# Sparse attention with two feed-forward layers in one launch: weight pieces three half-pieces ahead, a PSUM bank for the sums of squares, half-size weight loads and a planner with new latencies

## The chip, the cores and the metric

The kernel runs on one core of one Trainium2 chip. The metric is the device time of one execution in microseconds; the time before is the median of three runs. Engines are named as in the profile: PE is TensorE (PEld its weight loads), DVE is VectorE, ACT is ScalarE, POOL is GpSimd, SP is SyncE, which here issues all DMAs.

## What is computed

Top-32 attention over 4 batches of 8 heads, 576 rows of 64, and then two feed-forward layers over the 2304 rows. All inputs come in 64-bit floats.

```python
scores = scale * np.matmul(q, k.transpose(0, 1, 3, 2))
kth = np.partition(scores, -top_k, axis=-1)[..., -top_k:-top_k + 1]
scores = np.where(scores >= kth, scores, -1000000000.0)
attn = np.exp(scores - np.max(scores, axis=-1, keepdims=True))
attn = attn / (np.sum(attn, axis=-1, keepdims=True) + 1e-09)
x = np.matmul(attn, v)          # heads side by side: 2304 x 512
h = x @ w_in                    # 512 x 2048
x = np.maximum(0.01 * h, h) @ w_out
h = x @ w_in2
out = (h * (1.0 / (1.0 + np.exp(-h)))) @ w_out2
```

## The kernel before

The 2304 rows are cut into 18 blocks of 128 rows (one row block of each two batches is shared, 64 rows each), and a block's 8 heads into 4 pairs, so that attention has 72 pairs. A pair goes through: scores on PE (L760, into S), a copy to SBUF on ACT (L772), the search for the 32nd largest value on DVE (4 rounds of MAX8 and 3 of MATCH_REPLACE8 for each of the two heads, L784 to L788), bias on POOL (L798), cut and exponential on ACT (L810, L818), a split of the weights p into two 16-bit halves (ACT L833, POOL L841), a DMA transpose (L850) and the product with v on PE (L866). After 4 pairs a block is normed, split and transposed into xT, and the layers take it in quanta of 12 matmuls of 128x512 each: 4 quanta h0 (L978, from xT), 4 quanta o0 (L1031, into acc), the same again for layer 2 (h1 from yT, o1). Every product of two 32-bit values is made of 16-bit halves: high by high, high by low, low by high.

The weights are four matrices of a million values (w_in, w_out, w_in2, w_out2), each in 8 pieces of 128x1024. A piece is loaded as raw 64-bit words (L432), then ACT takes the upper word (L439), the top bits of the lower word are shifted down by ACT or DVE ("shift", L467 or L464), and DVE joins both ("join", L476), which gives a 32-bit float y. PE adds up the squares of all pieces (L493), DVE takes the trace and a scale (L503), and each piece is then scaled and split into a high half (ACT, L521 or L523) and a low half, made by DVE (L528) or by POOL (L533, behind a scaling by ACT L538 or POOL L540). All of this lies in one tile, w_all, in slots of 2048 16-bit columns: a piece's y lies one slot above the slot of its halves, so that the halves of piece g overwrite y of piece g-1. Raw words lie in free slots further up; the last two pieces of w_out2 go through 256-column loads into the one buffer `of`, and shifts of w_out2 into the three `g` buffers. Squares of q, x and the output of layer 1 (L682, L916) write into `junk`, a PSUM bank that only takes what nobody reads; the sums of squares of the weights use the PSUM tile `acc` of the second matmul.

The order of all instructions is set by a planner (Plan.run): operations are added with an engine, a duration, a latency and their names; the planner simulates five engines and the DMA queue, takes for each engine the candidate of the highest rank (the length of what depends on it, with PACE, plus BOOST) among those that can start within SLACK of the earliest, with LATE added to the readiness of some; the instructions are then issued engine by engine in that order, and nothing overtakes on an engine at run time. AHEAD holds layer 1 at most three blocks ahead of layer 2.

Of the kernel before, what the change touches and what calls it, by code (L numbers as in the profile page):

```python
# [31 lines left out]
NRAW = 4  # L32
W_AFTER = (("ktr", 0, 0), ("qtr", 0, 0))

W_MID = (
    ("ACT", "DVE", "ACT", "ACT", "ACT", "ACT", "ACT", "ACT"),
    ("ACT", "ACT", "ACT", "ACT", "ACT", "ACT", "ACT", "DVE"),
    ("ACT", "ACT", "ACT", "ACT", "ACT", "ACT", "DVE", "DVE"),
    ("ACT", "ACT", "DVE", "ACT", "ACT", "ACT", "ACT", "DVE"),
)  # L40
W_LO = (
    ("DVE", "ACT", "ACT", "ACT", "DVE", "ACT", "DVE", "ACT"),
    ("DVE", "ACT"),
    ("DVE", "ACT", "DVE", "POOL", "DVE", "ACT", "DVE", "POOL"),
    ("DVE", "ACT", "DVE", "ACT", "DVE", "ACT", "DVE", "ACT"),
# [1075 lines left out]
```

## Time and profile before

| | before |
|---|---|
| time, median of 3 runs (lowest to highest) | 1101.1 us (1099.29 to 1101.45) |
| profiled execution, its own time | 1101.91 us |
| its span, first to last instruction | 1100.1 us |
| busy: PE, DVE, ACT, POOL | 957.0, 896.0, 823.2, 637.4 us |
| mean granted clock of PE | 0.938 |
| HBM read, written | 47.71 MB, 4.72 MB |

The page gives busy time by engine; a group of instructions shows its count, busy time, mean duration and the idle time of its engine ahead of it with what ended it. Names in the rows: m and w are the search's tiles, sb the copied scores, ph and pT the split and transposed weights of attention, hl and gT the same of the layers, h and acc the layers' PSUM tiles.

### The profile page before, as it was taken

What the parts mean: (1) busy time and instruction counts of PE and PEld (TensorE: products, weight loads), DVE (VectorE), ACT (ScalarE), POOL (GpSimd) and SP (SyncE); (2) the same over time, 40 slices, a digit from 0 to 9 for tenths busy, and PEclk for the clock granted to TensorE, in tenths of its full rate; (3) what the DMA queues carried; (4) which work ended last, traced back from release to release, by engine and by line L of the source; (5) the groups of instructions that cost most, each with busy time, mean ns of one, the idle gap of its engine ahead of it and who ended that gap; (6) DMA issues with size and microseconds to landing.
All of it is one profiled execution on the core that took longest, in us unless ns stands there. A gap on an engine that the chain in (4) does not pass through costs nothing.

```text
span 1100.1 us, 19543 instructions
## 1 busy us (share of the span) xinstructions
PE 957.0 (87%) x6824; PEld 486.4 (44%) x6824; DVE 896.0 (81%) x1853; ACT 823.2 (75%) x1235; POOL 637.4 (58%) x913
## 2 busy tenths in 40 slices
PE   2434735668999999999999999999999999999998
PEld 1223313334554544544544545445454545444443
DVE  4999989998948999999999999994899999951010
ACT  5999998778866887878988778786787878662322
POOL 1355656567774776665876576665666665552321
PEclk9655867788999999999999999999999999999999
DMA  7997878553975687678888687687567766574432
GB/s 216 311 313 227 197 221 211 103 111 67 162 137 111 133 151 148 112 130 148 165 149 145 118 155 123 128 143 139 117 126 126 146 123 122 102 129 63 76 64 58
DMA packets 458115, 157.53 MB, mean 143 GB/s; under 512 B 440864, under 2 KB 449056, under 8 KB 455968
## 3 DMA queue, kind: packets, MB, share of 16 engines
q1 hardware_dynamic: 458016, 156.29, 70.0%
q8 instruction: 53, 0.87, 0.3%
q14 instruction: 46, 0.38, 0.1%
HBM read 47.71 MB, written 4.72 MB: 48 GB/s over the span
## 4 chain that ended last, share of the span: by engine, by line
PE 49%; DVE 20%; ACT 11%; issue 7%; POOL 6%; DMA 5%; SPq 1%; ACTq 0%; POOLq 0%; DVEq 0%
PE acc L1031 21%; PE h L978 20%; DVE w L786 7%; DVE m L788 6%; PE S L760 3%; PE pv L866 3%; POOL ph L841 2%; DMA pT<-ph 2%; ACT sb L818 2%; DVE w_all L476 2%; DVE m L784 1%; ACT sb L810 1%; POOL hl L1012 1%; ACT w_all L439 1%; PE acc L493 1%
## 5 line engine op out<-in xcount | busy, mean ns | idle before, releaser
L1031 PE MATMUL acc<-w_all,gT 128*128 128x512 f16 x1728 | 400.4, 382 | 12.8 <-ACT w_all L523 5.5
L788 DVE MAX8 m<-w 128x8 f32<-128x576 f32 x432 | 307.6, 746 | 0.0
L1012 POOL TENSOR_TENSOR hl<-g,hl 128x512 f16<-128x512 f32 x144 | 174.5, 1212 | 149.1 <-ACT hl L1005 132.3
L1031 PEld LDWEIGHTS <-gT 128*128 128x128 f16 x1728 | 166.3, 99 | 205.4 <-issue 18.3
L841 POOL TENSOR_TENSOR ph<-sb,ph 128x1152 f16<-128x1152 f32 x72 | 171.1, 2377 | 124.8 <-ACT ph L833 114.3
L786 DVE MATCH_REPLACE8 w<-m,w 128x576 f32<-128x576 f32 x288 | 212.1, 742 | 0.0
L978 PE MATMUL h<-w_all,xT 128*128 128x512 f16 x864 | 200.7, 384 | 12.7 <-DMA xT<-hlx 11.7
L978 PE MATMUL h<-w_all,yT 128*128 128x512 f16 x864 | 197.0, 381 | 0.6 <-DVE g L996 0.6
L760 PE MATMUL S<-k,qT 128*128 128x64 f16 (+3 forms) x640 | 94.2, 309 | 51.7 <-ACT sb L772 28.9
L978 PEld LDWEIGHTS <-xT 128*128 128x128 f16 x864 | 84.5, 99 | 113.9 <-DMA xT<-hlx 12.4
L818 ACT ACTIVATE sb<-sb,nb,u 128x576 f32<-128x576 f32 x144 | 122.5, 862 | 15.9 <-POOL nb L798 9.6
L978 PEld LDWEIGHTS <-yT 128*128 128x128 f16 x864 | 84.2, 98 | 99.5 <-issue 2.4
L996 DVE SCALAR_TENSOR_TENSOR g<-g,h 128x512 f32<-128x512 f32 x72 | 49.1, 682 | 95.9 <-ACT g L991 94.0
L810 ACT ACTIVATE sb<-sb,m 128x576 f32<-128x576 f32 x144 | 108.8, 764 | 24.4 <-DVE m L788 24.3
L772 ACT ACTIVATE sb<-S 128x1152 f32<-128x1152 f32 x72 | 81.0, 1125 | 46.5 <-POOL ph L841 44.7
L1005 ACT ACTIVATE hl<-g 128x512 f16<-128x512 f32 x144 | 89.8, 624 | 29.8 <-DVE g L996 25.0
L784 DVE MAX8 m<-sb 128x8 f32<-128x576 f32 x144 | 101.9, 745 | 6.4 <-ACT sb L772 6.3
L786 DVE MATCH_REPLACE8 w<-m,sb 128x576 f32<-128x576 f32 x144 | 105.9, 742 | 0.0
L866 PEld LDWEIGHTS <-pT 128*128 128x128 f16 (+1 forms) x2400 | 81.4, 104 | 29.1 <-DMA pT<-ph 13.7
L866 PE MATMUL pv<-v,pT 128*128 128x65 f16 (+3 forms) x2400 | 85.3, 199 | 9.4 <-DMA pT<-ph 9.3
L798 POOL TENSOR_SCALAR nb<-m,u 128x1 f32<-128x1 f32 x144 | 63.6, 445 | 49.3 <-DVE m L788 46.7
L760 PEld LDWEIGHTS <-qT 128*128 128x128 f16 (+1 forms) x640 | 44.5, 106 | 100.8 <-issue 45.6
(99 smaller groups left out, 1005.9 us busy)
## 6 DMA issues: line engine op xcount, KB each, us to landing
w_all<-in_moe_w_in_dram SPq DMA_DIRECT2D x16, 1024.0 KB, 6.3
w_all<-in_moe_w_out_dram SPq DMA_DIRECT2D x14, 1024.0 KB, 6.0
raw<-in_k_dram SPq DMA_DIRECT2D x16, 256.0 KB, 3.8
rawq<-in_q_dram SPq DMA_DIRECT2D x32, 128.0 KB, 2.8
raw<-in_v_dram SPq DMA_DIRECT2D x16, 256.0 KB, 3.1
out_dram<-of SPq DMA_DIRECT2D x16, 256.0 KB, 2.4
gT<-hl SPq DMA_TRANSPOSE x144, 3.2
of<-in_moe_w_out_dram SPq DMA_DIRECT2D x8, 256.0 KB, 2.8
```

Source lines behind the costliest of these rows:

```text
L760: nc.tensor.matmul(out=t[p0:p1, o:o + k1 - k0], lhsT=lhs, rhs=kt[:, k0:k1], start=(x == 0), stop=(x == 1),)
L784: nc.vector.max(m[:, 0], T[sbk][:, h])
L786: nc.vector.match_replace(w, m[:, step // 2], T[sbk][:, h] if step == 1 else w, NEG)
L788: nc.vector.max(m[:, step // 2], w)
L810: nc.scalar.activation(out=x, in_=x, func=AF.Prelu, scale=-1.0, bias=T["m", s][:, h, 3, 7:8], alpha=2.0**-CUT)
L818: nc.scalar.activation(out=x, in_=x, func=AF.Exp, scale=T["u", blk, hf][:, 1, p % 2:p % 2 + 1], bias=T["nb", s][:, h:h + 1],)
L841: nc.gpsimd.tensor_tensor(out=T[phk][:, 1, x0 * S:x1 * S], in0=T[sbk][:, x0:x1].rearrange("p h k -> p (h k)"), in1=T[phk][:, 0, x0 * S:x1 ...
L866: nc.tensor.matmul(out=o[p0:p1, 0:d1 - d0], lhsT=pT[:, c, p0:p1], rhs=T["v", b, p][:, vc, d0:d1], start=(i == 0), stop=(i == len(mm) - 1),)
L978: nc.tensor.matmul(out=t, lhsT=a[:, ai], rhs=w_rhs(layer, wi, kk, i), start=(n == 0), stop=(n == 3 * KDM - 1))
L1005: nc.scalar.activation(out=n[:, 0], in_=T[gk], func=AF.Copy)
L1012: nc.gpsimd.tensor_tensor(out=n[:, 1], in0=T[gk], in1=n[:, 0], op=ALU.subtract)
L1031: nc.tensor.matmul(out=t, lhsT=g[:, ai], rhs=w_rhs2(layer, wi, 4 * i + j), start=(i == 0 and j == 0 and n == 0), stop=(i == NCH - 1 and j ...
```

## The change

It changes seven things.

1. **Slots.** w_all is addressed in half-slots of 1024 columns. A piece's y now lies three half-slots (6 KB) above its halves, raw words in half-slots 51 to 66. The high half of piece g waits for the low half of piece g-2, the low half for that of g-1; so two pieces can be in work at once.
2. **Shift in place.** The shifted bits are written into the raw tile itself, in every second 32-bit word, by ACT, DVE or now POOL (from the 16-bit word, as ACT does).
3. **Who does what.** Tables W_MID, W_HI and W_LO: of the shifts of 1024 columns ACT had 20 and DVE 4; now ACT has 7, DVE 10, POOL 7. Of 512 columns ACT had 10, DVE 2; now ACT 2, DVE 4, POOL 7. Of 256: ACT 4, DVE 4; now POOL 6. DVE makes 18 low halves for 15, POOL 14 for 17; ACT scales 9 pieces for 15, POOL 5 for 2; POOL makes 3 of the 32 high halves. Joins on DVE: 24 of 1024, 12 of 512, 8 of 256 before; 24, 13 and 6 after.
4. **Loads.** 512 columns at a time (67 weight loads for 38), from the start of the program; the rest of w_out2 is staged in two `k` and `v` buffers in place of `of`; loads of k and v behind the first block wait until all weight loads are issued; the planner issues a weight load only when the DMA queue is within 0.5 us of empty.
5. **PSUM.** `junk` goes; a bank `gram` holds the sums of squares, which run piece by piece for all four matrices. Squares of q and x go into qT and xT, those of layer 1's output into `of`.
6. **Constants.** w_consts and u2 are made in two parts: layer 2's h needs the scales of three matrices only.
7. **Planner.** New durations and latencies; BOOST, PACE and LATE with other numbers and more names; NUDGE, a rank for single operations; TAIL and HOP for the time from an end to a waiting engine; a rule that an instruction of DVE on the list PORT, when POOL is busy by more than STALL, counts as starting at POOL's end, and POOL's next instruction as waiting for it.

```diff
-    "raw": 2, "rawq": 2, "g": 3, "of": 1, "hlk": 1, "hlx": 1, "hl": 2, "gT": 3, "xT": 1, "yT": 2, "xf": 1,
+    "raw": 2, "rawq": 2, "g": 2, "of": 1, "hlk": 1, "hlx": 1, "hl": 2, "gT": 3, "xT": 1, "yT": 2, "xf": 1,
...
-W_AFTER = (("ktr", 0, 0), ("qtr", 0, 0))
...
 BOOST = {
-    "g2": 200, "comb": 200, "norm": 200, "ylo": 200, "xlo": 200, "kvscale": 200, "wtrace": 200,
+    "g2": -1639, "comb": 1589, "norm": -1649, "ylo": 1315, "xlo": 583, "kvscale": -335, "wtrace": 200,
...
+NUDGE = {
+    290: -4105, 1074: -2255, 1097: -2285, 1239: -1961, 1818: -1479, 1200: 1526, 673: -1232, 923: -1982,
...
+TAIL = {"PE": 0.16, "ACT": 0.09, "DVE": 0.085, "POOL": 0.03, "SP": 0.0}
+HOP = {"PE": 0.055, "ACT": 0.036, "DVE": 0.036, "POOL": 0.085, "SP": 0.08}
+PORT = ("wjoin", "wlo", "kvlo", "xlo", "qlo", "wmid")
+STALL = 0.09
+AHEAD_DMA = 0.5
...
+                        if o.heavy:
+                            u = max(u, dma_free - AHEAD_DMA)
+                            t = max(t, dma_free - AHEAD_DMA)
+                        if e == "DVE" and o.port and clock["POOL"] > u + STALL:
+                            u = clock["POOL"]
+                        elif e == "POOL" and port_end > t:
+                            u, t = max(u, port_end), port_end
...
-    junk = ps.tile([128, 512], F32, name="junk", tag="junk", bufs=1)
+    gram = ps.tile([128, 128], F32, name="gram", tag="gram", bufs=1)
...
-    w_all = wp.tile([128, (4 * NWP + 1) * 2 * WP], F16, name="w_all")
+    w_all = wp.tile([128, (8 * NWP + 3) * WP], F16, name="w_all")
...
     def w_f32(i, c):
-        return w_at(NWP * i + c + 1).bitcast(F32)
+        return w_at(2 * (NWP * i + c) + 3, 2).bitcast(F32)
...
+                def mid(n=n, c=c, raw=raw):
+                    t = raw().rearrange("p (n t) -> p n t", t=2)[:, :, 0]
+                    m16 = raw().bitcast(U16).rearrange("p (n t) -> p n t", t=4)[:, :, 1]
+                    if mid_on(c) == "DVE":
+                        nc.vector.tensor_scalar(t, t, 29, None, op0=ALU.logical_shift_right)
+                    elif mid_on(c) == "POOL":
+                        nc.gpsimd.tensor_scalar(t, m16, 2.0**-13, -0.4999, op0=ALU.mult, op1=ALU.add)
...
-            yn = [n for d in (range(NWP) if i > 1 and c == 0 else [c]) for n in w_names(d)]
-            add("PE", 0.5, square, r=yn, w=[("gram", i)], new=[("acc", ("gram", i))] if c == 0 else [], name=f"gram{i}")
+            add("PE", 0.46, square, r=w_names(c), w=["gram"], name=f"gram{i}", seq="gram")
...
+            add(hi_on(c), 0.96 if hi_on(c) == "ACT" else 1.2, hi, r=yn + [("ws", i), ("wlo", g - 2)], w=[("whi", g)], name=f"whi{i}")
+            add("POOL" if plain else "DVE", 2.12 if plain else 1.19, lo,
+                r=[("ws", i), ("whi", g), ("wlo", g - 1)], w=yn + [("wlo", g), ("w", i, c)], name=f"wlo{i}")
...
-                out=junk[:, 0:256], in_=T[rk].rearrange("p h d -> p (h d)"), func=AF.Square,
```

How it moves instructions, at three places. First DVE at the start of the program, behind v's first low half: L642 and L694 split k and v, L476 and L532 are joins, L464 and L520 shifts, L784 and L836 the first step of the first search. Before:

```order
L642 SCALAR_TENSOR_TENSOR v<-raw,sv_75,v 128x9x64
L356 TENSOR_SCALAR fx<-h 128x1
L357 TENSOR_SCALAR sk_71<-fx 128x1
L358 TENSOR_SCALAR sk_71<-fx 128x1
L784 MAX m_187<-sb 128x8 x2
L642 SCALAR_TENSOR_TENSOR hlk<-raw,sk_71,hlk 128x9x64
```

After:

```order
L694 SCALAR_TENSOR_TENSOR v<-raw,sv_75,v 128x9x64
L532 SCALAR_TENSOR_TENSOR w_all<-w_all 128x1024
L766 SCALAR_TENSOR_TENSOR hlx<-rawq,qs,hlx 128x4x64 x2
L520 TENSOR_SCALAR w_all<-w_all 128x1024
L411 TENSOR_SCALAR fx<-h 128x1
L412 TENSOR_SCALAR sk_71<-fx 128x1
L413 TENSOR_SCALAR sk_71<-fx 128x1
L532 SCALAR_TENSOR_TENSOR w_all<-w_all 128x1024
```

The first search stood right behind the second scale of k; now joins and shifts stand ahead of it, four and three by the time it comes (two of them ahead of these rows).

Second, DVE at the first joins of w_out2. Before:

```order
L357 TENSOR_SCALAR sv_76<-fx 128x1
L358 TENSOR_SCALAR sv_76<-fx 128x1
L476 SCALAR_TENSOR_TENSOR w_all<-w_all,g 128x512 x3
L464 TENSOR_SCALAR g<-w_all 128x512 x2
L476 SCALAR_TENSOR_TENSOR w_all<-w_all,g 128x512 x3
```

After (L550 is the trace of w_in2, L586 a low half):

```order
L520 TENSOR_SCALAR w_all<-w_all 128x512
L532 SCALAR_TENSOR_TENSOR w_all<-w_all 128x512
L836 MAX m_1208<-sb 128x8
L550 SCALAR_TENSOR_TENSOR gram,wtot<-gram,ident 128x128
L836 MAX m_1208<-sb 128x8
L532 SCALAR_TENSOR_TENSOR w_all<-w_all 128x512 x2
L586 SCALAR_TENSOR_TENSOR w_all<-w_all,ws_911 128x1024
L532 SCALAR_TENSOR_TENSOR w_all<-w_all 128x512 x4
```

Three joins and three more stood there with two shifts between; now there are one, two and four, with search steps, a trace and a low half between them.

Third, SP at the start of the program, where L432 and L500 load weights, L597, L601, L649 and L653 load k and v, L673 and L725 q. Before:

```order
L597 DMA raw<-in_k_dram 128x2x256
L601 DMA raw<-in_k_dram 64x64 x2
L673 DMA rawq<-in_q_dram 128x4x64
L597 DMA raw<-in_v_dram 128x2x256
L601 DMA raw<-in_v_dram 64x64 x2
L673 DMA rawq<-in_q_dram 128x4x64
L660 DMA_TRANSPOSE k<-hlk 128x9x128
```

After:

```order
L500 DMA w_all<-in_moe_w_in_dram 128x1024
L649 DMA raw<-in_k_dram 128x2x256
L653 DMA raw<-in_k_dram 64x64 x2
L500 DMA w_all<-in_moe_w_in_dram 128x1024
L725 DMA rawq<-in_q_dram 128x4x64
L649 DMA raw<-in_v_dram 128x2x256
L653 DMA raw<-in_v_dram 64x64 x2
L500 DMA w_all<-in_moe_w_in_dram 128x1024
```

The first weight load stood behind the first transposes and the second k and v; now it is the first DMA, and one stands between each of the others.

## Rows read from the trace of the kernel before

**Rows 1.** The page, busy time of each engine, share of the span, instructions

```profile
PE 957.0 (87%) x6824; PEld 486.4 (44%) x6824; DVE 896.0 (81%) x1853; ACT 823.2 (75%) x1235; POOL 637.4 (58%) x913
```

**Rows 2.** Three stretches by windows; each engine's busy time, clock, DMA

```profile
core 0: us, PE busy (x) PEld busy (x) DVE busy (x) ACT busy (x) POOL busy (x), PEclk, DMA share, GB/s
0.00:297.90 297.90, 168.16 (x1247) 96.15 (x1248) 269.03 (x509) 251.71 (x349) 170.08 (x216) 0.78 0.75 195
297.90:976.40 678.50, 668.87 (x4972) 335.11 (x4972) 614.89 (x1326) 531.29 (x822) 431.54 (x657) 1.00 0.74 133
976.40:1100.10 123.70, 120.01 (x608) 55.18 (x606) 12.06 (x20) 40.18 (x65) 35.76 (x41) 1.00 0.41 72
```

**Rows 3.** PE's timeline around 257 and 297 us: start, us, line, idle before

```profile
257.57 2.08 PE L760 MATMUL S<-k,qT 128*128 128x512 f16 x8 [5.19 <-ACT sb L772]
...
296.67 1.21 PE L760 MATMUL S<-k,qT 128*64 128x512 f16 x16
```

**Rows 4.** The chain of waits, 170 to 300 us: start, us, what

```profile
243.63 5.01 PE acc L493 x64
...
285.32 2.59 PE h L978 x12
```

**Rows 5.** Groups of DVE's instructions to 297.9 us: busy, mean ns, idle before

```profile
L476 DVE SCALAR_TENSOR_TENSOR w_all<-w_all 128x1024 int32<-128x1024 int32 x24 | 32.5, 1362 | 0.1
...
L528 DVE SCALAR_TENSOR_TENSOR w_all<-w_all,ws 128x1024 f16<-128x1024 f32 x15 | 24.0, 1602 | 1.8 <-ACT w_all L523 1.8
L476 DVE SCALAR_TENSOR_TENSOR w_all<-w_all,g 128x512 int32<-128x512 int32 x12 | 10.3, 891 | 5.3 <-ACT g L467 5.1
L476 DVE SCALAR_TENSOR_TENSOR w_all<-w_all,g 128x256 int32<-128x256 int32 x8 | 9.0, 1124 | 0.1
...
L464 DVE TENSOR_SCALAR g<-of 128x256 int32<-128x256 int32 x4 | 3.5, 882 | 0.0
...
L464 DVE TENSOR_SCALAR w_all<-w_all 128x1024 int32<-128x1024 int32 x4 | 2.7, 684 | 0.0
...
L464 DVE TENSOR_SCALAR g<-w_all 128x512 int32<-128x512 int32 x2 | 0.8, 422 | 0.0
```

**Rows 6.** The same lines: duration ns min/median/max, first and last start

```profile
L476 DVE SCALAR_TENSOR_TENSOR w_all<-w_all x24: 1193/1210/3084, 23.8 to 150.4; 128x1024 int32<-128x1024 int32 x24
L476 DVE SCALAR_TENSOR_TENSOR w_all<-w_all,g x20: 403/690/2414, 159.9 to 228.0; 128x512 int32<-128x512 int32 x12, 128x256 int32<-128x256 int32 x8
...
L528 DVE SCALAR_TENSOR_TENSOR w_all<-w_all,ws x15: 1259/1278/2437, 68.2 to 276.6; 128x1024 f16<-128x1024 f32 x15
...
L464 DVE TENSOR_SCALAR g<-of x4: 285/666/1910, 208.6 to 225.4; 128x256 int32<-128x256 int32 x4
```

**Rows 7.** DVE's timeline: start, us, line, and the idle time before it

```profile
17.35 0.16 DVE L356 TENSOR_SCALAR fx<-h 128x1 int32<-128x1 int32 x1 [5.30 <-PE h L551]
...
159.91 2.83 DVE L476 SCALAR_TENSOR_TENSOR w_all<-w_all,g 128x512 int32<-128x512 int32 x3 [5.13 <-ACT g L467]
...
173.15 1.29 DVE L476 SCALAR_TENSOR_TENSOR w_all<-w_all,g 128x512 int32<-128x512 int32 x2
...
297.10 0.75 DVE L788 MAX8 m<-w 128x8 f32<-128x576 f32 x1
```

**Rows 8.** Groups of POOL's instructions to 297.9 us

```profile
L533 POOL TENSOR_TENSOR w_all<-w_all 128x1024 f16<-128x1024 f32 x17 | 37.4, 2200 | 27.1 <-ACT w_all L521 24.9 <-issue 2.0
...
L540 POOL TENSOR_TENSOR w_all<-w_all,ws 128x1024 f32<-128x1024 f32 x2 | 4.4, 2204 | 0.0
```

**Rows 9.** Groups of ACT's instructions to 297.9 us

```profile
L467 ACT ACTIVATE w_all<-w_all 128x1024 int32<-128x1024 uint16 x20 | 22.4, 1123 | 3.2 <-DMA w_all<-in_moe_w_in_dram 3.0 <-DVE w_all L476 0.2
```

**Rows 10.** Who waited for whom, DVE to 297.9 us: total, times, longest

```profile
DVE fx L356 <- PE h L551: 12.6, 5, 5.8
...
DVE junk L503 <- PE acc L493: 2.2, 2, 1.8
```

**Rows 11.** The page, DMA issues: KB each, us to landing

```profile
w_all<-in_moe_w_in_dram SPq DMA_DIRECT2D x16, 1024.0 KB, 6.3
```

More of the change, by code (lines that the diff above doesn't have):

```diff
@@ L80 @@
+SLACK = {
+    "PE": 0.03, "ACT": 0.14, "DVE": 0.08, "POOL": 0.02, "SP": 0.1,
+}
 STATS = {}
@@ L86 @@
 class Op:
-    __slots__ = ("n", "eng", "dur", "lat", "dma", "fn", "new", "use", "pred", "succ", "bl", "left", "ready", "t0", "t1", "name", "soft", "stage", "slot")
+    __slots__ = ("n", "eng", "dur", "lat", "dma", "fn", "new", "use", "pred", "succ", "bl", "left", "ready", "t0", "t1", "name", "soft", "stage", "slot", "port", "tr", "heavy")
 class Plan:
@@ L159, in run @@
         engines = ("PE", "ACT", "DVE", "POOL", "SP")
-        clock = {e: 0.0 for e in engines}
+        turn = False
+        clock = {e: 0.7 for e in engines}
         busy = {e: 0.0 for e in engines}
         dma_free = 0.0
+        port_end = 0.0
         cand = {e: [] for e in engines}
@@ L177, in run @@
             best = None
-            for e in engines:
+            for e in ("PE", "ACT", "POOL", "DVE", "SP") if turn else engines:
                 lst = []
@@ L398, in w_rows, with w_units @@
         return w_bits[i][kk * 128:(kk + 2) * 128, :].rearrange("(k p) d -> p k d", p=128)
-    def slot(j):
-        return ("slot", j)
+    RAW3 = (53, 55, 57, 59, 61, 63, 65, 59, 61, 63, 65, 63, 65)
+    STAGE = ("k", "v")
+    def w_units(i, c):
+        if i < 3:
+            return [(0, WP, 51 + 4 * (c % 4))]
+        out = []
+        for h in range(2):
+            n = 2 * c + h
+            if n < len(RAW3):
+                out.append((512 * h, 512, RAW3[n]))
+            else:
+                out += [(512 * h + o, 256, STAGE[o // 256 % 2]) for o in (0, 256)]
+        return out
     def w_ops(i):
@@ new lines, in w_ops, with load @@
+                step = min(n, 512)
+                for o2 in range(0, n, step):
+                    def load(o=o, o2=o2, n=n, c=c, home=home, rk=rk, raw=raw, step=step):
+                        if home == "k":
+                            T[rk] = tile_of(rk, "k", [128, 9 * 128], F16)[:, 0:1024].bitcast(I32)
+                        elif home == "v":
+                            T[rk] = tile_of(rk, "v", [128, 10 * VW], F16)[:, 0:1024].bitcast(I32)
+                        nc.sync.dma_start(out=raw()[:, 2 * o2:2 * (o2 + step)], in_=w_rows(i, c, o + o2, step))
+                    k = o2 // 512 * 2
+                    add("SP", 0.42, load, w=rn[k:k + 2] + tn[k:k + 2], new=rnew, lat=2.4, dma=2.7 * step / WP,
+                        name=f"wload{i}", seq="wload", mark="wlast")
@@ new lines, in w_ops, with join @@
+                add(mid_on(c), {"DVE": 0.08 + 0.52 * n / WP, "ACT": 0.1 + 0.92 * n / WP, "POOL": 0.1 + 1.1 * n / WP}[mid_on(c)], mid,
+                    w=tn, name=f"wmid{i}")
+                def join(o=o, n=n, c=c, raw=raw):
+                    y = w_f32(i, c).bitcast(I32)[:, o:o + n]
+                    t = raw().rearrange("p (n t) -> p n t", t=2)[:, :, 0]
+                    nc.vector.scalar_tensor_tensor(
+                        out=y, in0=y, scalar=3, in1=t, op0=ALU.logical_shift_left, op1=ALU.bitwise_or
+                    )
```

398 lines of the change are left out of this document (196 added, 202 removed), and 10 rows, old and new, of tables (BOOST, LATE).

## The prediction

> **What bounds the kernel now.** I began with the shares on the page: PE is busy for 87% of the span and DVE for 81% [rows 1]. Neither number decides anything, since both are averages, so next I cut the span at two instants of DVE's timeline. One is 297.9 us, where DVE ends the top-32 search of pair 17 (a pair is one 128-row block with two heads; there are 72). The other is 976.4 us, where it ends pair 72. The reader should compare the three rows [rows 2]. Before 297.9, PE works for 168 of 298 us at a mean granted clock of 0.78 (it moves between the two levels 1.2 and 2.4 GHz), while DVE works for 269.0. After it, PE has 668.9 of 678.5 and then 120.0 of 123.7, at clock 1.00. So the last 802 us are PE's own work: 788.9 of 802.2 busy, some 13 us to be had there by anyone. The first 298 us are DVE's. That DVE is 615 of 678 busy in the middle matters little: its waits there are for PE.
>
> The timeline of PE joins the two stretches [rows 3]. Its last long wait, 5.19 us before the scores at 257.6, is for the copy of earlier scores; from there it runs without a gap. A quantum (12 matmuls of 512 columns, either layer's h or acc) costs 2.59 us, as the chain of waits shows [rows 4]. There are 288. In the listed order of PE's instructions 29 stand ahead of the scores of pair 18 (at 296.7). So a microsecond that DVE saves before pair 18 is worth a microsecond at the end, as long as PE's order keeps about the same number of quanta behind that point. In the changed order 28 stand ahead instead of 29: one quantum more is left, **+2.6 us**.
>
> **DVE up to pair 17.** 269.0 busy and 28.9 idle. The change doesn't touch the search. It touches the weights: 7 groups of rows, 32.5+24.0+10.3+9.0+3.5+2.7+0.8 = 82.8 us [rows 5]. How much of it is work? The smallest durations say [rows 6]: a join of 1024 takes 1.193, one of 256 0.403, a low half 1.259, a shift of 256 0.285; two joins of 512 in 1.29 give 0.645 [rows 7]; shifts of 1024 and 512 have tight means, 0.684 and 0.422 [rows 5]. Alone, the present work is 24x1.193 + 12x0.645 + 8x0.403 = 39.5 for joins, 15x1.259 = 18.9 for low halves, 4x0.684 + 2x0.422 + 4x0.285 = 4.7 for shifts: 63.1. The other 19.7 us are instructions that were stretched (a join took up to 3.084).
>
> The change makes joins 24x1.193 + 13x0.645 + 6x0.403 = 39.4, low halves 18x1.259 = 22.7, shifts 10x0.684 + 4x0.422 = 8.5: 70.6, **+7.5 us**. DVE gets more work, not less. The shifts now write every second word in place; no row shows this. If the stride halved their rate, they would cost 8.5 more. I take no change, since they already read with that stride; the 8.5 stays in the range.
>
> **The stretch.** What becomes of the 19.7? In the big joins it is 32.5-28.6 = 3.9 on 28.6, 14%; in the 256-wide ones 5.8 on 3.2, and those stand among the 2.2 us subtractions of POOL [rows 8]. The new planner delays DVE's instructions of this kind until POOL is through, or takes a search step instead, and only 6 joins of 256 are left. I take the big joins' 14% for all: 9.6, **-10.1 us**. From below it can go to 0 (-19.7). From above: 69 such instructions become 75 (+9%), and POOL gets 12 pieces' worth of shifts (7 of 1024, 7 of 512, 6 of 256), 8 scalings for 2, and 14 subtractions for 17. No row shows a POOL scaling or shift of this form; it lies between DVE's 0.684 and POOL's 2.204 [rows 5, 8]. That makes 14x2.200 + 20x0.684 to 20x2.204 = 44.5 to 74.9 us for 37.4+4.4 = 41.8, POOL's 170 us up by 2 to 19%. 19.7x1.09x1.19 = 25.6, +5.9. POOL itself has over 95 idle us of 298 to hide it in.
>
> The rows show joins between 1.193 and 3.084 us while POOL's two-input subtractions last 2.200 [rows 6, 8]: that is a block, not a slower rate. The Trainium skill ("Perfetto Trace Analysis", Optimizing Scalar/DVE Operations) says that GpSimd and DVE share a read port, so that moving work from one to the other "might not help"; by that the +5.9 end holds, by the big joins' row -10.1.
>
> **The idle time.** Three waits of DVE lose their cause. At 159.9 it waits 5.13 us for ACT's shifts [rows 7]; ACT had 20 such of 1024, 22.4 us [rows 9], and keeps 7; the joins after it now get theirs mostly from POOL and DVE. At 17.35 it waits 5.30 us for a sum of squares [rows 7]; in the changed order four joins, three shifts and more stand ahead of the first search (the first order excerpt). At w_out2's trace it waits up to 1.8 us for PE [rows 10], which runs 64 squares at once (5.01 us, [rows 4]) because acc is taken; with a bank of their own they run piece by piece and 8 are left at the end, under 0.7 us. Sum **-12.2 us**. Bounds: 0, if others take their place, to -23.1, if only the opening 5.8 [rows 10] remains of 28.9. The first k now queues behind a weight load of half a MB; one MB lands in 6.3 us [rows 11], so it costs between 0 and 3.2. I take a quarter, **+0.8**, since DVE's opening wait also holds the load of k itself and ACT's first pass.
>
> **Edits that I cost at nothing.** ACT loses 13 shifts of 1024, 14.6 us by [rows 9], and some scalings; it works for 252 of 298 [rows 2], and the waits for it are counted above. SP issues 67 weight loads for 38; its queue holds them between transposes, and the loads now wait for a short queue. That is covered as long as DMA keeps up: its share is 0.75 [rows 2], and without that cover the gain in idle time goes first. The squares of q and x now write the tile that the transpose fills later: they wait for PE to be done with it. For q that is the scores two pairs back, about 2x12.3 us earlier (678.5 us for 55 pairs, [rows 2]); without this cover pair 18 is late. Two-deep slots (6 KB) let a high half start before the last low half ends; DVE's own waits for it are 1.8 us, ACT's are off the path. The constants in two parts let layer 2 start without w_out2; PE's order still puts its first h behind the last squares.
>
> **Sum.** 7.5 - 10.1 - 12.2 + 0.8 = -14.0 up to the end of pair 17 (297.9 now [rows 7], 283.9 then), +2.6 for the quantum: -11.4. The profiled execution took 1101.9 us (span 1100.1 and 1.8 around it), so 1090.5; it lay 0.8 above the median, so **1089.7 us** against 1101.1. All best ends give -19.7+7.5-23.1+2.6 = -32.7 (1068), all worst +7.5+5.9+3.2+2.6 = +19.2 (1120), and 8.5 more with the stride.
>
> **Rivals.** (a) The waits go further down, because the planner now reckons with landing times from a trace: stretch near 0 and idle time at 12 to 14. For it: of 28.9 idle us the opening 5.8 and the three waits leave 10.9 in small pieces that a better order could fill. Against: more loads go through the 16 DMA engines that are at 0.75 already. 7.5-19.7-16+0.8+2.6 = -24.8: 1076, within 1068 to 1079. Chance 0.20.
> (b) No change: DVE is earlier, but PE can't use it. Between pairs 12 and 18 PE needs the low halves of w_out2, and the last of 18 falls behind pair 15 as before; PE then waits for them, and the quanta left at 297.9 are the same. For: PE's wait of 5.19 at 257.6 [rows 3] shows it starving just there. Against: 28 quanta are ordered ahead, and squares end sooner. 1099 to 1103. Chance 0.10.
> (c) Slower: **the shared port**. DVE's and POOL's weight work meet more often, and the stretch rises instead of falling. Price +7.5+5.9 with one idle wait gone (-5.1) and +2.6: +10.9, 1112. The Trainium skill's sentence on the read port ("Perfetto Trace Analysis", Optimizing Scalar/DVE Operations) would lead one to expect this case. It decides from a stretch of 19.7-(7.5+2.6-5.1) = 14.7 us on: above that the new order loses more than that wait brings. For: the 3.084 us joins. Against: the planner's rule for such instructions, fewer narrow joins. Chance 0.15; 0.05 more for worse (an order with little slack, late at every step).
>
> **Numbers.** Forecast 0.50 (1079 to 1099). A measurement of this kernel can tell 0.2%, 2.2 us, from no change. Faster: 0.50 + 0.20 + 0.02 of (b) = 0.72; same 0.08, from (b)'s middle and the edge of (c); slower 0.20. The range 1068 to 1112 leaves out the worse half of (c) and what lies behind it; the likeliest case alone is 1079 to 1099.
>
> **What would show it.** Pair 17's search ends near 284 (right), under 275 (a), over 300 (c). The stretch: the 1024 joins at a mean of 1.36 or under (c: above 1.5). DVE's idle time up to there near 17. PE gapless from pair 18, about 805 us long. If pair 17 is early and the end isn't, (b). If the stretch behind pair 18 is shorter than 795, my claim that it is PE's own work falls.

## The result, and the profile after

The changed kernel takes 1072.7 us (median of 4 runs, 1070.6 to 1074.1) against 1101.1: ratio 0.9744, interval 0.9725 to 0.9763, 28.4 us faster. The forecast was 11.4 us faster with a range of 1068 to 1112: the direction was right, the size less than half. The profiled execution took 1074.1 us, its span is 1072.4 (before 1101.9 and 1100.1).

The page of the changed kernel, busy time of each engine, and its three stretches by windows (columns as there), cut as in [rows 2] where DVE ends pairs 17 and 72:

```profile
PE 947.5 (88%) x6824; PEld 482.0 (45%) x6824; DVE 881.8 (82%) x1859; ACT 792.6 (74%) x1206; POOL 653.5 (61%) x936
```

```profile
0.00:287.00 287.00, 170.33 (x1291) 96.47 (x1292) 263.36 (x517) 227.11 (x320) 192.04 (x238) 0.80 0.81 203
287.00:942.30 655.30, 650.93 (x4901) 327.67 (x4900) 606.21 (x1325) 523.26 (x818) 423.32 (x651) 1.00 0.76 137
942.30:1072.40 130.10, 126.25 (x636) 57.90 (x634) 12.22 (x19) 42.26 (x70) 38.13 (x47) 1.00 0.39 73
```

Against [rows 1], PE makes the same 6824 matmuls in 9.5 us less, and is idle for 1072.4-947.5 = 124.9 instead of 143.1 us. So 18 of the 28 us are PE's waits; the other 9.5 are work that took less time. How much of that comes from TensorE's clock isn't shown. The mean granted clock (between the levels 1.2 and 2.4 GHz) was higher between 150 and 200 us, where PE had more to do, 0.83 (below, the second row) in place of 0.67 (the first), but lower in the first 150 us, 0.69 in place of 0.73.

```profile
150.00:200.00 50.00, 21.59 (x199) 14.60 (x196) 43.68 (x79) 42.19 (x68) 29.95 (x49) 0.67 0.73 204
```

```profile
150.00:200.00 50.00, 34.11 (x279) 18.29 (x276) 49.90 (x104) 41.67 (x62) 39.09 (x51) 0.83 0.70 159
```

DVE ends pair 17 at 287.0, 10.9 earlier; forecast were 14.0. It is idle for 287.0-263.4 = 23.6 us up to there (28.9 before, 17.5 forecast).

DVE's groups that treat weights, up to 287.0 us (busy, mean ns of one, idle time before it):

```profile
L532 DVE SCALAR_TENSOR_TENSOR w_all<-w_all 128x1024 int32<-128x1024 int32 x24 | 31.7, 1326 | 0.6 <-ACT w_all L508 0.6
L586 DVE SCALAR_TENSOR_TENSOR w_all<-w_all,ws 128x1024 f16<-128x1024 f32 x18 | 26.9, 1495 | 0.2 <-ACT w_all L579 0.2
...
L532 DVE SCALAR_TENSOR_TENSOR w_all<-w_all 128x512 int32<-128x512 int32 x13 | 8.7, 694 | 0.0
L520 DVE TENSOR_SCALAR w_all<-w_all 128x1024 int32<-128x1024 int32 x10 | 7.2, 725 | 4.8 <-DMA w_all<-in_moe_w_in_dram 4.8
...
L532 DVE SCALAR_TENSOR_TENSOR w_all<-w_all,v 128x256 int32<-128x256 int32 x3 | 1.7, 571 | 0.0
L520 DVE TENSOR_SCALAR w_all<-w_all 128x512 int32<-128x512 int32 x4 | 1.7, 417 | 2.2 <-DMA w_all<-in_moe_w_out_dram 2.2
L532 DVE SCALAR_TENSOR_TENSOR w_all<-w_all,k 128x256 int32<-128x256 int32 x3 | 1.5, 516 | 0.0
```

They sum to 79.4 us for 82.8 in [rows 5]. Alone this work is the forecast's 70.6, so the stretch is 8.8 (19.7 before, 9.6 forecast). The shifts kept their rate although they now write every second word: nine of the ten of 1024 columns take 0.66 to 0.70 us, one 1.09. Two idle times are new: 4.8 and 2.2 us in which DVE waits for the load of a weight.

Who waited for whom, DVE of the changed kernel to 287.0 us (total, times, longest):

```profile
DVE fx L411 <- PE h L600: 9.3, 3, 7.7
DVE w_all L520 <- DMA w_all<-in_moe_w_in_dram: 4.8, 4, 2.0
DVE w_all L520 <- DMA w_all<-in_moe_w_out_dram: 2.2, 1, 2.2
...
```

Now PE. Who waited for whom between 200 us and the point from which it runs on without a long wait, first before (200 to 257.7), then after (200 to 275):

```profile
PE S L760 <- ACT sb L772: 14.2, 3, 6.8
PE h L978 <- DMA xT<-hlx: 7.6, 1, 7.6
PE pv L866 <- DMA pT<-ph: 2.2, 1, 2.2
PE S L760 <- DMA qT<-hlx: 0.9, 1, 0.9
```

```profile
PE h L600 <- DVE g L1054: 2.9, 1, 2.9
PE S L812 <- ACT sb L824: 1.1, 2, 0.6
PE acc L1089 <- DVE w_all L586: 1.0, 1, 1.0
...
```

PE's timeline after, the scores of pairs 16 and 18:

```profile
247.77 1.14 PE L812 MATMUL S<-k,qT 128*128 128x512 f16 x8
...
272.80 1.19 PE L812 MATMUL S<-k,qT 128*64 128x512 f16 x16 [0.48 <-ACT sb L824]
```

This is where the forecast's link breaks. Pair 18's scores come at 272.8 in place of 296.7 [rows 3], 23.9 us earlier, although DVE's pair 17 is only 10.9 earlier. In PE's order 21 quanta stand ahead of pair 16's scores (17 before) and 28 ahead of pair 18's (29 before). Below, a kernel's place at a pair is measured as the start of the last of that pair's score matmuls (0.7 to 0.8 us behind the first) minus 2.59 us for each quantum ahead of them, and its lead is the difference of two kernels: 222.4 before and 201.1 after at pair 18, a lead of 21.3 us; 18.5 at pair 22; 20.4 at pair 28; 28.0 at pair 72.

### The profile page after: what moved, and what is told of

The parts are those of the page before. It is cut to its first block, busy times and chain, and to the rows that moved or that the text cites. A ratio compares the mean times of both kernels' runs of the same rounds, so it can differ in the third digit from the quotient of the medians.

```text
span 1072.4 us, 19725 instructions
## 1 busy us (share of the span) xinstructions
PE 947.5 (88%) x6824; PEld 482.0 (45%) x6824; DVE 881.8 (82%) x1859; ACT 792.6 (74%) x1206; POOL 653.5 (61%) x936
## 4 chain that ended last, share of the span: by engine, by line
PE 52%; DVE 22%; ACT 8%; DMA 7%; POOL 5%; issue 4%; SPq 2%; DVEq 0%; ACTq 0%; POOLq 0%
PE acc L1089 23%; PE h L1036 22%; DVE w L838 7%; DVE m L840 6%; PE pv L918 3%; PE S L812 3%; DVE w_all L532 2%; DVE m L836 2%; DMA w_all<-in_moe_w_in_dram 2%; POOL ph L893 2%; DMA pT<-ph 2%; DVE w_all L586 2%; ACT sb L862 1%; DMA qT<-hlx 1%; ACT sb L824 1%
## 5 line engine op out<-in xcount | busy, mean ns | idle before, releaser
L1070 POOL TENSOR_TENSOR hl<-g,hl 128x512 f16<-128x512 f32 x144 | 168.5, 1171 | 126.9 <-ACT hl L1063 114.4
L812 PE MATMUL S<-k,qT 128*128 128x64 f16 (+3 forms) x640 | 90.0, 300 | 26.9 <-ACT sb L824 20.4
L836 DVE MAX8 m<-sb 128x8 f32<-128x576 f32 x144 | 101.8, 745 | 12.3 <-ACT sb L824 12.3
L918 PEld LDWEIGHTS <-pT 128*128 128x128 f16 (+1 forms) x2400 | 80.4, 103 | 24.8 <-DMA pT<-ph 11.2
L885 ACT ACTIVATE ph<-sb 128x1152 f16<-128x1152 f32 x72 | 83.2, 1155 | 2.2 <-DMA pT<-ph 1.2
```

Source lines behind the costliest of these rows:

```text
L812: nc.tensor.matmul(out=t[p0:p1, o:o + k1 - k0], lhsT=lhs, rhs=kt[:, k0:k1], start=(x == 0), stop=(x == 1),)
L836: nc.vector.max(m[:, 0], T[sbk][:, h])
L918: nc.tensor.matmul(out=o[p0:p1, 0:d1 - d0], lhsT=pT[:, c, p0:p1], rhs=T["v", b, p][:, vc, d0:d1], start=(i == 0), stop=(i == len(mm) - 1),)
L1070: nc.gpsimd.tensor_tensor(out=n[:, 1], in0=T[gk], in1=n[:, 0], op=ALU.subtract)
```

## The experiments

Times in us, medians; "before" is the kernel before, run beside them. Differences in the text are those of the medians.

| run | time | before | ratio, 95% interval |
|---|---|---|---|
| b_short_late | 1100.6 | 1100.8 | 0.9998, 0.9989 to 1.0007 |
| b_short_early | 1098.7 | 1100.8 | 0.9983, 0.9974 to 0.9993 |
| b_short_first | 1099.5 | 1102.2 | 0.9970, 0.9956 to 0.9984 |
| b_split | 1102.6 | 1100.8 | 1.0022, 1.0013 to 1.0031 |
| b_split_pin | 1100.4 | 1100.9 | 0.9997, 0.9987 to 1.0006 |
| b_split_pin33 | 1097.7 | 1102.2 | 0.9958, 0.9942 to 0.9975 |
| b_then_a | 1099.6 | 1100.9 | 0.9989, 0.9977 to 1.0000 |
| b_then_a28 | 1095.5 | 1102.2 | 0.9932, 0.9918 to 0.9947 |
| b_split_then_a | 1092.2 | 1102.2 | 0.9906, 0.9891 to 0.9920 |
| a_hold7 | 1099.3 | 1100.8 | 0.9987, 0.9976 to 0.9997 |
| a_late_old | 1098.2 | 1100.9 | 0.9973, 0.9960 to 0.9986 |
| a_nudge0 | 1108.7 | 1100.9 | 1.0062, 1.0043 to 1.0080 |
| b_mid_pool | 1107.3 | 1101.1 | 1.0058, 1.0043 to 1.0073 |
| b_mid_pool_short | 1106.3 | 1101.1 | 1.0047, 1.0032 to 1.0062 |
| a_mid_act | 1076.0 | 1101.1 | 0.9776, 0.9759 to 0.9792 |
| a_dose | 1085.4 | 1101.1 | 0.9854, 0.9838 to 0.9871 |
| a_dve2act | 1072.1 | 1101.2 | 0.9742, 0.9728 to 0.9757 |
| a_dve2act_w | 1072.3 | 1101.2 | 0.9747, 0.9732 to 0.9763 |

### Does the end hang on DVE? Three shortened searches

In the kernel before, with its order, two pairs lose the middle of their searches:

```diff
+                if s + 1 in (16, 17) and 2 <= step <= 5:
+                    return
                 if step == 0:
                     nc.vector.max(m[:, 0], T[sbk][:, h])
```

(12, 13) in b_short_early, (5, 6) in b_short_first.

b_short_late: 

> The kernel before, order unchanged; the searches of pairs 16 and 17 leave out their middle four steps per head (top 16 in place of top 32 for these two pairs), so DVE has 16 steps of about 0.69 us less, 11 us, and ends pair 17 near 287 in place of 297.9. Theory P17 (the forecast's own link: the end hangs on DVE's end of pair 17): -11, near 1090. Theory P16 (PE is the bound from the scores of pair 16, at 257.6, because it runs without a gap from there; what counts is when those scores start and how many quanta stand ahead of them): DVE's gain comes too late to be used, 0 to -2, 1099 to 1101.

b_short_early: 

> The kernel before, order unchanged; the same 16 steps, 11 us, are left out of the searches of pairs 12 and 13 instead (top 16 in place of top 32 there). Theory P17: -11, near 1090, the same as for the late pairs. Theory P16: DVE is ahead of the scores of pair 16 by then, these start up to 11 us sooner, and PE's idle time between the scores of pair 13 (221) and those of pair 16 (257.6) shrinks: -8 to -11, 1090 to 1093.

b_short_first: 

> The kernel before, order unchanged; the middle four steps per head of the searches of pairs 5 and 6 are left out (top 16 in place of top 32 there): 11 us less of DVE's work between 81 and 120 us. For pairs 12 and 13 the same 11 us gave 2, for pairs 16 and 17 nothing. Theory D (DVE is the bound only until about pair 10, and the kernel of that time is in-order waits of ACT, POOL and PE afterwards): -7 to -11, 1090 to 1094. Rival N (DVE is not the bound there either): 1098 to 1101. The forecast's link says 1090.

Eleven us less of DVE's work gave 0.2, 2.1 and 2.7 us. So theory P17, the forecast's link, is wrong, and theory D (DVE is the bound until pair 10) with it: at none of the three places in this order was DVE's time the bound by itself. For the late pairs DVE's waits show why (b_short_late, 257.6 to 298 us), and its timeline:

```profile
DVE fx L356 <- PE h L551: 6.2, 1, 6.2
DVE den L885 <- PE pv L868: 3.4, 1, 3.4
...
```

```profile
296.45 0.16 DVE L356 TENSOR_SCALAR fx<-h 128x1 int32<-128x1 int32 x1 [6.17 <-PE h L551]
```

The first step, -11 at pair 17, failed too: DVE ended it at 297.5. In its list stand instructions that need a sum from PE, and PE gives that sum only behind its quanta. PE's timeline is that of the kernel before:

```profile
257.32 2.08 PE L760 MATMUL S<-k,qT 128*128 128x512 f16 x8 [5.19 <-ACT sb L772]
...
296.34 1.20 PE L760 MATMUL S<-k,qT 128*64 128x512 f16 x16
```

So DVE's end of pair 17 follows PE, not the other way round. For pairs 12 and 13 theory P16 expected -8 to -11 and missed: pair 13 ended 9.2 us sooner, but pair 16's scores only 2.2, and the end followed these. What holds them is in the chain of waits of the kernel before:

```profile
249.98 0.06 DVE fx L356
...
250.06 0.17 DVE ws L357
...
250.25 1.15 ACT w_all L523
251.40 1.91 ACT w_all L538 x2
...
253.38 1.04 ACT w_all L521
254.42 2.08 ACT w_all L538 x2
256.50 1.02 ACT sb L772
...
257.57 0.59 PE S L760
```

The copy of pair 15's scores stands in ACT's order behind six passes over w_out2, and these wait for w_out2's scale, at 250. In the changed kernel that weight's squares are summed at 218.2 in place of 248.7. For pairs 5 and 6, DVE's idle time up to pair 17 rose by 7.6 of the 11 us; its waits there (b_short_first, 80 to 200 us) are for ACT's passes over weights, of which only the first and 1.5 us of the second were in the kernel before:

```profile
DVE w_all L476 <- ACT g L467: 5.1, 1, 5.1
DVE w_all L528 <- ACT w_all L523: 4.7, 3, 3.1
DVE w_all L476 <- ACT w_all L439: 2.8, 2, 1.4
DVE w_all L476 <- ACT w_all L467: 1.4, 1, 1.4
...
```

### Layer 2's first quanta: the constants in two parts

b_split is the kernel before with the change's w_consts and u2_make:

```diff
-            add("POOL", 0.9, w_consts, r=[("ws", i) for i in range(4)], w=[("wc",)], name="w_consts")
+            add("POOL", 0.6, lambda: w_consts(False), r=[("ws", i) for i in range(3)], w=[("wc", 0)], name="w_consts")
+            add("POOL", 0.3, lambda: w_consts(True), r=[("ws", 3), ("wc", 0)], w=[("wc", 1)], name="w_consts")
```

> The kernel before with one thing of the change: the constants in two parts, so that layer 2's first matmuls need the scales of three weights and only the store of the result needs w_out2's. In its listed order 21 quanta in place of 17 stand ahead of the scores of pair 16. Theory P16: these four quanta go into PE's idle time before 257.6, 4 x 2.59 = 10.4 us: near 1091, DVE's end of pair 17 about where it was. Rival F (layer 2 is held up by something else, its weights' low halves say, so PE cannot fill the gap): no change, 1099 to 1103. Rival D (all of the change's gain is DVE's): no change.

It was slower by 1.8 us, which no theory had. The trace shows the expected filling: 21 quanta ahead of pair 16's scores, a lead of 11.2 us at pair 18. But the planner makes the whole list anew after any edit, and the new list behind lost it: 7.1 at pair 22, 2.4 at pair 64. So the next two runs keep the order of the kernel before behind a joint, a place in the list of all operations up to which one order stands and from which another's is written out:

```diff
+        place = {n: i for i, n in enumerate(REST)}
+        order[1793:] = sorted(order[1793:], key=lambda o: place[o.n])
...
+REST = (
...
+)
```

b_split_pin (joint at operation 1249): 

> The kernel before with the constants in two parts, as in the run on that alone, but with an order written out: up to the scores of pair 22 that run's order, behind them the order of the kernel before. In that run the scores of pair 22 came at 353.1 us with 50 quanta ahead of them, in the kernel before at 357.7 with 49: by (time minus 2.59 x quanta) it was 7.1 us ahead, and lost it behind pair 56. Theory K (PE is the bound from there and keeps a lead unless the order behind is worse): -7, near 1094. Theory Z (a lead of PE alone is given back in any order, because DVE's pairs are no earlier): 1099 to 1102.

b_split_pin33: 

> Again the kernel before with the constants in two parts, its own order in front and the order of the kernel before behind, now joined behind the scores of pair 33, where both orders have issued the same operations but one, so that the joint itself should cost nothing (at pair 22 it cost 8.6 us at once, so that run could not tell). At pair 32 the run with the split was 6.2 us ahead by (time minus 2.59 x quanta). Theory K (a lead of PE is kept if the order behind is the same): -6, 1094 to 1096. Theory Z (it is given back in any order): 1099 to 1102.

The joint at pair 22 was bad: the lead was gone within one pair, 5.0 us of it in a wait of PE for a step of ACT that now stood elsewhere. The joint at pair 33 gave -4.4 us: theory K, a little under its size. So in the kernel before layer 2's early start is worth about 4 us, provided that nothing behind takes it back. What it is worth in the changed kernel is less plain: there w_out2's scale is made at 222.2 us (250.1 before), 5.5 us ahead of layer 2's first quantum (227.7), so that the earlier squares by themselves may have allowed much of it; no run separates the two. The reverse, on the changed kernel:

```diff
-        add("PE", 2.59, h_quantum, r=[ak] + ... + [("u2", blk)] * layer, w=[hk],
+        add("PE", 2.59, h_quantum, r=[ak] + ... + [("u2", blk)] * layer + [("w", 3, c) for c in (0, 1, 2, 3, 4, 5, 6, 7) if layer and blk == 0], w=[hk],
```

a_hold7: 

> The changed kernel with one dependence more: the first layer-2 block's matmuls wait for the low half of w_out2's last piece (268 us in the changed kernel's trace), as if the constants were late. In its listed order 16 in place of 21 quanta stand ahead of the scores of pair 16. Theory P16: five quanta more are left from there, +13: near 1086. Theory D (the gain is DVE's alone): DVE's work is the same, so no change, 1071 to 1075. Rival O (any edit makes the planner's order worse, whatever it is): slower, but with pair 16's scores later rather than fewer quanta ahead of them.

It lost 26.6 us against the changed kernel, twice the expectation: 14.7 by pair 22, near the 13 of theory P16, the other half behind, in a list made anew. Layer 2's first quantum comes at 270.7 us here, 43 us later than in the changed kernel (late constants alone leave it at 249.6 in the kernel before); so this run shows that the early start counts, and not the price of the two parts.

### The order behind pair 22 or 28

b_then_a and b_then_a28 are joints of the same kind on the code of the kernel before, with the changed kernel's order behind (operations 1245 and 1575); b_split_then_a does it to b_split (1629).

b_then_a: 

> The kernel before, its own code and its own order up to the scores of pair 22, behind them the order of the changed kernel. (Time minus 2.59 x quanta) grows from pair 22 to pair 72 by 115.6 us in the kernel before and by 106.1 in the changed one. Theory L (that part of the gain, 9.5 us, is the order behind pair 22 alone): near 1091.5. Rival M (it comes from the code of the change, squares that no longer share one PSUM bank, say, or from the earlier start): 1099 to 1103.

b_then_a28: 

> Again the kernel before, its code and order in front and the changed kernel's order behind, now joined behind the scores of pair 28, where the two orders differ by 5 operations. From pair 28 to pair 72 (time minus 2.59 x quanta) grows by 99.1 us in the kernel before and by 91.5 in the changed one. Theory L (that difference is the order alone, on the old code): -7.6, near 1093. Rival M (it needs the code of the change, or its earlier start): 1099 to 1102.

b_split_then_a: 

> Both: the kernel before with the constants in two parts and its own order up to pair 29's scores, the changed kernel's order behind. By K and L together: the 6 to 7 us that the split is ahead at pair 28 to 32 and the 7.6 of the order behind: 1086 to 1089. If only one of them holds, 1093 to 1095; if neither, 1099 to 1102.

The first joint was bad again (the time less the quanta grew by 8.1 us from pair 22 to 23, by 2.4 in the kernel before), and the run gave 1.3 in all. The second is clean: -6.6 us, theory L. Windows from pair 28's scores to the end, of the kernel before, of b_then_a28 and of the changed kernel (which has one quantum less left):

```profile
425.90:1100.10 674.20, 663.98 (x4601) 328.04 (x4599) 522.75 (x1111) 473.36 (x728) 385.50 (x563) 1.00 0.68 122
```

```profile
426.20:1094.10 667.90, 661.04 (x4601) 327.78 (x4599) 516.65 (x1111) 469.17 (x728) 381.18 (x563) 1.00 0.68 123
```

```profile
408.10:1072.40 664.30, 658.56 (x4589) 326.34 (x4587) 514.58 (x1109) 469.82 (x733) 383.15 (x575) 1.00 0.68 123
```

The same 4601 matmuls take 6.3 us less in another order, 3.4 of it PE's idle time (10.2 to 6.9) and 2.9 PE's work, for which the windows show no cause. Both parts together gave -9.9 us, less than their sum and more than either.

The other direction, on the changed kernel:

```diff
+            if o.name == "S" and sum(x.name in ("S", "S!") for x in order) == 22:
+                late, boost, nudge, slack = LATE2, BOOST2, {}, SLACK2
```

a_late_old (LATE2, BOOST2 and SLACK2 are the tables of the kernel before): 

> The changed kernel, its order untouched up to the scores of pair 22; behind them the planner goes on with the lateness, boost and slack numbers of the kernel before and no nudges. Theory L: the 9.5 us behind pair 22 are the numbers', so up to +9.5: 1079 to 1083. Rival M (code): 1071 to 1075.

```diff
-NUDGE = {
-    290: -4105, 1074: -2255, 1097: -2285, 1239: -1961, 1818: -1479, 1200: 1526, 673: -1232, 923: -1982,
...
+NUDGE = {}
```

a_nudge0: 

> The changed kernel with the table of 19 single nudges empty, nothing else: the same instructions on the same engines, in another order (22 in place of 21 quanta ahead of the scores of pair 16, 28 ahead of pair 18's as now). Theory S (the gain is what the code does: shifts, pieces, bank, loads): 1070 to 1078. Theory R (most of the gain is the order that these numbers pick): over 1085, with DVE's search of pairs 10 to 14 or PE's start without gaps later.

With the old numbers behind pair 22 the changed kernel loses 25.5 us, nearly its whole gain; windows from pair 22's scores to the end, a_late_old and the changed kernel:

```profile
337.30:1094.60 757.30, 733.61 (x5135) 362.17 (x5133) 583.51 (x1261) 530.24 (x824) 431.99 (x649) 0.99 0.68 122
```

```profile
339.10:1072.40 733.30, 725.95 (x5135) 360.47 (x5133) 583.33 (x1261) 527.44 (x824) 430.28 (x649) 1.00 0.69 126
```

The matmuls and the instructions of the other engines are the same in number; PE's idle time is 23.7 in place of 7.4 us and its work 7.7 longer. Without the 19 nudges the changed kernel is slower than the kernel before, by 36 us against itself: 11.2 lost by pair 22, the rest behind. Theory R holds: the same code in another list gives all of the gain away. Both runs change some of the planner's numbers and leave the others, so they show how much a list can cost, not how much of the 28.4 us the good one brought.

### What a microsecond of DVE, ACT and POOL is worth

The kernels here keep their lists; only the engine that does a step differs, or one step is added.

```diff
+                            if i < 3:
+                                nc.gpsimd.tensor_scalar(t_of(), m16[:, o2:o2 + m], 2.0**-13, -0.4999, op0=ALU.mult, op1=ALU.add)
+                                return
                             nc.scalar.activation(
```

b_mid_pool: 

> The kernel before, list order unchanged; the 20 shifts of 1024 of w_in, w_out and w_in2 that ACT does (22.4 us) run on POOL at the same places of the list. In the kernel before ACT is busy for 95.8 us of those from 50 to 150, DVE for 97.0. Theory C (DVE and ACT hold each other up there: to relieve one alone gains little): -2 to -5, 1096 to 1099. Rival A (ACT alone is the bound there): -8 to -15, 1086 to 1093. Rival P (POOL's shifts stretch DVE's joins, the shared port): 1103 or more.

b_mid_pool_short (pairs 5 and 6 shortened too): 

> Both at once: the shifts on POOL and the searches of pairs 5 and 6 cut to the top 16 (11 us less for DVE, which alone gave 2.7). Theory C: clearly more than the sum of the two alone, -8 to -14, 1087 to 1093. If the two simply add: 1094 to 1097. If neither is the bound: 1097 to 1101.

Both slower, in the range of rival P. DVE's groups to 305 us in b_mid_pool, and POOL's shifts:

```profile
L479 DVE SCALAR_TENSOR_TENSOR w_all<-w_all 128x1024 int32<-128x1024 int32 x24 | 32.3, 1354 | 1.5 <-POOL w_all L468 1.4
L531 DVE SCALAR_TENSOR_TENSOR w_all<-w_all,ws 128x1024 f16<-128x1024 f32 x15 | 25.9, 1726 | 2.4 <-ACT w_all L526 2.4
...
L464 DVE TENSOR_SCALAR w_all<-w_all 128x1024 int32<-128x1024 int32 x4 | 4.6, 1139 | 0.0
```

```profile
L468 POOL TENSOR_SCALAR w_all<-w_all 128x1024 int32<-128x1024 uint16 x20 | 26.1, 1307 | 8.6 <-DVE w_all L479 3.6 <-DMA w_all<-in_moe_w_in_dram 3.0 <-DVE w_all L464 0.7
```

Pair 17 ends 4.7 us later and the kernel 6.3; DVE's work on the weights is 3.0 us longer (85.8 for 82.8). But the joins, which rival P has stretched, take 32.3 us for 32.5 [rows 5]. What grew are the low halves (1726 ns for 1602) and the shifts, and the mean of 1139 ns for 684 is one shift of four: it took 2.51 us, from 97.67, beside a subtraction of POOL (96.76 to 99.63); the other three took 0.68 to 0.69. The three longest low halves (2.39 to 3.19 us) also began beside two-input instructions of POOL. So most of DVE's stretch that the trace shows lies beside POOL's two-input work, and not beside its shifts; what in POOL's new load costs the 6.3 us wasn't tried. Theory C couldn't be judged, since POOL's price came in between; the 11 us less of search gave 1.1 us here (1107.3 to 1106.3).

```diff
-                        nc.gpsimd.tensor_scalar(t, m16, 2.0**-13, -0.4999, op0=ALU.mult, op1=ALU.add)
+                        nc.scalar.activation(out=t, in_=m16, func=AF.Copy, scale=2.0**-13, bias=-0.4999)
```

a_mid_act: 

> The changed kernel, list order unchanged; its 20 shifts on POOL (7 of 1024, 7 of 512, 6 of 256) run on ACT instead, some 13.6 us more for ACT, which is busy for 112 of the first 150 us. Theory C: ACT becomes the second bound again and part of the early gain goes, +5 to +13, 1078 to 1086. Rival Q (ACT has room for it): 1071 to 1075.

+3.3 us against the changed kernel: less than C, more than Q. ACT is busy for 11.6 us more (13.6 expected), POOL for 16.2 less; the move as a whole costs 0.3 us for each microsecond that ACT has more.

```diff
+                    if i in (1, 2):
+                        nc.vector.max(dose, w_f32(i, c)[:, 0:576])
```

a_dose: 

> The changed kernel, list order unchanged; behind each of the 16 joins of 1024 of w_out and w_in2 DVE makes one more step like the search's (a maximum over 576 elements whose result nobody uses), 16 x 0.68 = 10.9 us before about 150. Theory D (a microsecond of DVE there is a microsecond at the end): +9 to +12, 1082 to 1085. Rival W (DVE's time is not what counts there either): +0 to +3.

+12.7 us, theory D. DVE's groups that differ most, to 300 us:

```profile
L533 DVE SCALAR_TENSOR_TENSOR w_all<-w_all 128x1024 int32<-128x1024 int32 x24 | 34.7, 1444 | 0.6 <-ACT w_all L509 0.6
...
L537 DVE MAX8 dose<-w_all 128x8 f32<-128x576 f32 x16 | 12.2, 761 | 0.6
```

DVE's work grew by more than the new steps: the joins take 34.7 us for 31.7, and DVE is busy for 14.2 us more in all. This run is the cleanest cut through the result. DVE ends pair 17 at 297.6, the time of the kernel before (297.9), so its lead is taken away; yet the kernel is still 15.7 us faster than before. In the changed order taking DVE's lead away costs 12.7 of the 28.4 us; something else carries the rest. The other direction doesn't follow: in the order before, 11 us less of DVE's work gave at most 2.7.

Last, the attempt at a faster kernel, DVE's shifts on ACT:

```diff
-                    if mid_on(c) == "DVE":
+                    if mid_on(c) == "DVE" and i > 3:
```

a_dve2act: 

> The changed kernel, list order unchanged; all 14 shifts of weights that DVE does (10 of 1024, 4 of 512: 8.9 us) run on ACT instead, some 13 us more for ACT, which was busy for 112 of the first 150 us. A microsecond more for DVE there cost 1.1 at the end. Theory D both ways (DVE's time there is worth it in both directions): -5 to -9, 1064 to 1068, faster than both kernels. Theory O (a list that was made for these durations loses by a delay anywhere, and gains little by an instruction less): -2 to +4, 1071 to 1077.

a_dve2act_w (`i not in (1, 2)`): 

> The same for the five shifts of w_out and w_in2 alone (3.4 us of DVE's time between 45 and 130 us), where DVE doesn't wait for loads. Theory D: -2 to -4, 1069 to 1071. Theory O: 1072 to 1075.

No change, within theory O: with 8.9 us less work DVE in a_dve2act waits 9.3 us for ACT's passes before joins and ends pair 17 at 286.4. So DVE's time wasn't freed, and the run doesn't price it. In a_dve2act_w pair 17 ended at 283.1, but in the fastest of five executions that lie between 1070.6 and 1075.7 us; its median, 0.3 us under the changed kernel's, can't tell theory D's -2 from nothing. No run here beats the changed kernel clear of the noise.

## Why the prediction was too small

1. **The step that failed** is the link from DVE to the end: "a microsecond that DVE saves before pair 18 is worth a microsecond at the end", with 28 in place of 29 quanta ahead of pair 18's scores, "+2.6". The same section says, from [rows 3], that PE runs without a gap from 257.6. Then PE is the bound from pair 16's scores on, the quanta are to be counted there, and the order of the change has 21 ahead of them for 17: -10.4 in place of +2.6. DVE's pair 17 was the wrong instant; b_short_late shows that it follows PE, and none of the three shortened searches brought more than 2.7 of 11 us. At pair 16 the trace has both parts: scores 9.8 us earlier (257.6 to 247.8) and four quanta more behind PE, together 20 of the 21.3 us of lead at pair 18.
2. **"the last 802 us are PE's own work"**, with "some 13 us to be had there by anyone": the sum put nothing for them. b_then_a28 has 6.6 us from the order alone, about half of them PE's idle time. My mark for this (under 795 from pair 18's scores) wasn't reached, 1072.4-272.8 = 799.6 with one quantum more; the mark was too coarse.
3. **The constants in two parts, costed at nothing** because "PE's order still puts its first h behind the last squares". The reason came true (the last squares of w_out2 run at 210.0, layer 2's first quantum at 227.7), but it doesn't make the cost nothing: the squares are done 38 us earlier than before (248.6), and in the kernel before, with its late scales, the two parts alone are worth 4.4 us (b_split_pin33).
4. **DVE's idle time** was forecast to fall by 11.4 and fell by 5.3. The wait for ACT's shifts and the one for the squares are gone as said. The opening wait is 7.7 us, not 5.8 and a quarter of 3.2 (a weight load of half a MB lands in 5.7 us in the median, where I took half of the 6.3 for one MB), and DVE now waits 7.0 us for loads: I had covered SP's 67 loads at no cost.
5. **Right**: the weights' work (79.4 us for 80.2 forecast), the stretch (8.8 for 9.6), the shifts' rate, pair 17's end within 3.1 us. So DVE's part of the sum, -14.0 us, came to -10.9.
6. **Rivals.** (a) had the nearest time, 1076, but by luck: the stretch is not near 0, nor is DVE's idle time at 12 to 14. (b), that PE can't use DVE's lead, is wrong: PE used more. (c), the shared port, did not come: the stretch fell from 19.7 to 8.8 us. Its mechanism is there in part: in b_mid_pool POOL's shifts in a list not made for them cost 6.3 us, with 3.0 us more of DVE's work on the weights. The Trainium skill's sentence ("Perfetto Trace Analysis", Optimizing Scalar/DVE Operations) that offloading between GpSimd and DVE, which share a read port, "might not help" was not tested as it stands, since the shifts came from ACT. That the planner's rule for such steps lowered the stretch was not tried by itself.

The sum now: DVE's lead 12.7 (a_dose), layer 2's early start 4.4 and the order behind pair 28 6.6 make 23.7 of 28.4 us. The two last together gave 9.9, not 11.0, so some 5 to 6 us stay open; they lie by pair 28, where the changed kernel leads by 20.4 us. These three prices come from different lists, the first from the changed kernel's and the others from that of the kernel before, so that they add up is argued, not shown. What the two traces alone show is where the lead arises: 20.2 us of it by pair 16 and 7.6 behind pair 28. How much of the 12.7 each of bank, two-deep slots, short loads and POOL's shifts brought wasn't tried.

## What to carry to other kernels

Look for the instant from which the bound engine no longer waits, and count there what stands ahead of it; an engine that looks busy before that may itself be following. Where a planner writes the list, price the idle time of the bound engine in the whole program as something the new list can take or give: here the same instructions ran in 1072 to 1109 us. In these lists 14 us added to DVE cost 12.7 us (a_dose), and 11 taken away gave at most 2.7 (the shortened searches), since other engines' steps stood where they had been; so an experiment on a part needs the rest of the order held fixed.

## What the runs showed of the hardware

POOL's shift of 1024 elements from 16 to 32 bits takes 1.13 us in the median of b_mid_pool's 20 and 1.10 to 1.13 in five of the changed kernel's seven. The means are 1307 and 1345 ns, since some are held up: the changed kernel's shift from 122.33 us took 1.96, beside a DVE join that ran from 121.98 to 123.31. The reverse is there too: in b_mid_pool a DVE join from 139.46 took 1.91 us (1.21 alone), beside a POOL shift from 139.16 to 140.29. So POOL's one-input shift and DVE's two-input join get in each other's way. A shift of DVE beside a shift of POOL stands in none of these rows.

POOL's scaling as one-input form with a scale per partition takes 1117 ns (5 of 1024 in the changed kernel), where the two-input form with a broadcast took 2204 [rows 8]. DVE's shift that writes every second word in place took 725 ns on average, 0.66 to 0.70 us in nine of ten, no more than before (684).
